# A list that orders the first stage reckons with shorter TensorE turns and scores

## The chip, the cores and the metric

The kernel runs on one core of a Trainium2 chip. The metric is the time of one execution on the device, in microseconds. Three runs of the kernel before took 1630.80, 1632.95 and 1636.01 us; their median is 1632.95.

The engines are named as in the profile: PE is TensorE, which multiplies matrices (PEld its loading of weights), DVE is VectorE, ACT is ScalarE, POOL is GpSimd and SP is SyncE. ACT, POOL and SP also issue transfers between the chip's memory and the on-chip buffers.

## The reference

Attention over keys and values that are means of eight rows, and then two layers:

```python
k_p = k.reshape(B, H, Sp, pool, D).mean(axis=3)      # 576 rows -> 72
v_p = v.reshape(B, H, Sp, pool, D).mean(axis=3)
scores = scale * np.matmul(q, k_p.transpose(0, 1, 3, 2))
attn = np.exp(scores - max) ; attn = attn / (attn.sum() + 1e-09)
x = np.matmul(attn, v_p)                             # 8 batches, 8 heads, 576, 64
x = x.transpose(0, 2, 1, 3).reshape(4608, 512)
h = np.maximum(x @ w_in, 0.0)                        # 512 -> 2048
x = h * h @ w_out                                    # 2048 -> 512
h = x @ w2_in                                        # 512 -> 2048
out = np.maximum(0.01 * h, h) @ w2_out               # 2048 -> 512
```

All data are 32-bit floats; q and k are drawn eight times larger than v.

## The kernel before

A number enters a matrix product as a high and a low part, so that a product is three matmuls: high by high, high by low and low by high. The program has three stages, and the change lies in the first.

**The first stage** (0 to 564 us of the span) computes the attention and the first product of layer 1, block by block: nine blocks of 512 tokens. For a block, q comes in tiles of 128 tokens. TensorE turns a tile of q (L716), multiplies it with the turned, pooled keys (the scores, L764, in two halves), DVE takes the maximum (L774), ACT the exponentials (L786), DVE divides by the sums (L803 to L805) and copies the last keys (L819); TensorE turns the probabilities (L846, the last keys L853), ACT and DVE split these into high and low (L857/L860, L870/L875), and four kinds of value products (L919 to L922) give x, which ACT and DVE split again (L931/L935). The keys of each batch are pooled by DVE, turned by TensorE (L580, the last ones L586) and copied out (L592, L594); the values are pooled (L507), their rest is summed on TensorE (L532), and before they are used DVE puts their three splits into the buffers v_hi, v_lo and v_rem (L650), of which there is one each. Since 576 is no multiple of 512, a block has parts ("pieces") of two batches, and a tile can lie across both.

Then come sixteen **units** for each block: a unit is twelve matmuls of 128x512 (L1064) in four parts of three, into one of four accumulator banks (acc). ACT takes its relu (L1075) and its square (L1078), POOL stores it (L1094), and DVE adds the squares of neighbours (L1101), which POOL stores too (L1104). All other TensorE results pass through four banks named ps.

In the same stage forty **stored** jobs bring the weights of the later products into the form in which they are used: ACT takes an exponent (L242), DVE four bit steps (L246, L249, L260, L263), an addition (L1581) and sums into the single buffer wo3 (L429), which POOL writes out (L431). At its end it loads and splits the eight weight tiles of the next stage (L1767, L1773 on ACT, L1775 on DVE) and prepares three of its groups of tokens (L1736, L1754, L1758).

**What sets the order.** Each engine runs its instructions in the order of its list, and waits where a result or a buffer is not there. The first 16 units and the attention around them are issued by hand. Everything later in the stage, from about 110 us on, is put in order by the planner (`Plan.run`): each step has an engine, an estimated duration in us, a rank, the steps it follows and the buffers it takes. The planner takes, again and again, the step that can start earliest by its own clock (and among those the one of the lowest rank: values and chains of work first, then probabilities, scores, turns, pooling, sums, units, and the stored jobs last), gives it that start, and moves the engine's clock on by its duration. Its clock serves only for the order. The estimates are the second argument of `self.op`.

**The later stages**: the second product of layer 1 (L1800, 564 to about 900 us), in groups of tokens, each prepared by sums (L1736), a cast on ACT (L1754) and low parts on DVE (L1758); and layer 2 (L2021, then L2264), to the end of the span. The change does not touch their order.

Of the kernel before, what the change touches and what calls it, by code (L numbers as in the profile page):

```python
# [45 lines left out]
def attention_relu2_leaky_kernel(  # L46
# [109 lines left out]
    def taken(key):  # L156
        raws.pop(key)
# [1157 lines left out]
    class FirstStage:  # L1315
# [25 lines left out]
        def add_keys(self, b, rank):  # L1341
            rows, tail, kp, km, kl, kt = (
                Buffer(t) for t in ("wo4", "raw", "kp", "gh", "km", "kt")
            )
            load = self.dma(
                lambda: load_to(("k", b, "rows"), k_load_all(b), "wo4", (P, 4, 512)),
                rank, self.ROWS, gets=[rows])
            load_tail = self.dma(
                lambda: load_to(("k", b, "tail"), k_load(b, KEYS // P), "raw"), rank, self.TAIL, gets=[tail])
            steps = []  # L1350
            x = load
            for n, us in enumerate((1.22, 0.69, 0.43)):
                def fn(n=n):
                    if n == 0:
                        steps.extend(k_pool_rows(b))
                    steps[n]()
                after = [x, self.scored.get(b - 2)] if n == 0 else [x]
                x = self.op("DVE", us, fn, rank, after=after, gets=[kp] if n == 0 else (), uses=[rows, kp])
            y = self.op("DVE", 1.03, lambda: k_pool_tail(b), rank, after=[load_tail, x], uses=[tail, kp])
            masks = []  # L1360

            def mask(n):
                if n == 0:
                    masks.extend(k_mask_parts(b))
                masks[n]()

            x = self.op("DVE", 0.68, lambda: mask(0), rank, after=[x, y], gets=[km, kl], uses=[kp])
            y = self.op("DVE", 0.28, lambda: mask(1), rank, after=[x, y], uses=[kp, kl])
            parts = []

            def turn(n):
                if n == 0:
                    parts.extend(k_transpose_parts(b))
                parts[n]()

            p0, p1 = Buffer("ps"), Buffer("ps")
            t0 = self.op("PE", 0.63, lambda: turn(0), rank, after=[x, y], gets=[p0, kt], uses=[km])
            c0 = self.op("DVE", 0.69, lambda: turn(1), self.CHAIN, after=[t0], uses=[p0, kt])
            t1 = self.op("PE", 0.2, lambda: turn(2), rank, after=[y, t0], gets=[p1], uses=[kl])
            c1 = self.op("DVE", 0.22, lambda: turn(3), self.CHAIN, after=[t1, c0], uses=[p1, kt])  # L1380
            self.keys[b] = [c0, c1], kt

# [58 lines left out]
        def add_attention(self, blk):  # L1441
            t0 = blk * T
            self.last = []
            probabilities, pbuf = [], Buffer("pt")
# [5 lines left out]
            before = None  # L1450
            for i in tiles:
                for b, *_ in parts_of(i):
                    if b not in keyed:
                        keyed.add(b)
                        self.add_keys(b, self.POOLING)
                two = len(parts_of(i)) - 1
                raw, qt, ps = Buffer("raw"), Buffer("qt"), Buffer("ps")
                x = self.dma(lambda i=i: load_to(("q", i), q_load(i), "raw"), self.POOLING, self.QUERY,
                             n=1 + two, gets=[raw])
                qp = q_transpose_parts(i)  # L1460

                def copy(i=i, fn=qp[1]):
                    fn()
                    taken(("q", i))

                x = self.op("PE", 0.6, qp[0], 3, after=[x, self.tile.get(i - 2)], gets=[ps, qt], uses=[raw])
                x = self.op("ACT", 0.58, copy, self.CHAIN, after=[x], uses=[ps, qt])
                s, l, m = Buffer("s"), Buffer("l"), Buffer("m")
                after = [x]
                for b, *_ in parts_of(i):  # L1470
                    after += self.keys[b][0] if b in self.keys else []
                kts_ = [self.keys[b][1] for b, *_ in parts_of(i) if b in self.keys]
                exps = []
                for hf in range(2):
                    products, top, ex = score_parts(i, hf)
                    bank_ = Buffer("ps")
                    x = self.op("PE", 0.65 * (1 + two), products, 2, after=after,
                                gets=[bank_] + ([s, l, m] if hf == 0 else []), uses=[qt, *kts_])
                    self.tile[i] = x
                    for b, *_ in parts_of(i):  # L1480
                        self.scored[b] = x
                    after = [x]
                    y = self.op("DVE", 0.46, top, self.CHAIN, after=[x], uses=[bank_, m])
                    exps.append(self.op("ACT", 1.2, ex, self.CHAIN, after=[y], uses=[bank_, s, l, m]))
                whole, last_keys = normalize_parts(i)
                prem = Buffer("prem")
                x = self.op("DVE", 1.15, whole, self.CHAIN, after=exps, uses=[s, l])
                y = self.op("DVE", 0.36, last_keys, self.CHAIN, after=[x], gets=[prem], uses=[s])
                pe, high, low, pe_rem, high_rem, low_rem = p_parts(i, blk)
                b0, b1 = Buffer("ps"), Buffer("ps")  # L1490
                x = self.op("PE", 0.6, pe, 1, after=[x, y, before], gets=[b0] + ([] if before else [pbuf]),
                            uses=[s, pbuf])
                before = x
                h = self.op("ACT", 0.6, high, self.CHAIN, after=[x], uses=[b0, pbuf])
                lo = self.op("DVE", 0.69, low, self.CHAIN, after=[h], uses=[b0, pbuf])
                x = self.op("PE", 0.19, pe_rem, 1, after=[x, y], gets=[b1], uses=[prem])
                hr = self.op("ACT", 0.46, high_rem, self.CHAIN, after=[x], uses=[b1, pbuf])
                lr = self.op("DVE", 0.42, low_rem, self.CHAIN, after=[hr], uses=[b1, pbuf])
                probabilities.append([lo, lr])
            x_buf = self.x_buf[blk] = Buffer(f"x{blk % 2}")  # L1500
            ready = [[] for _ in range(KC)]
            for nb, b in enumerate(batches_of(t0)):
# [4 lines left out]
                for cc in range(KC):  # L1507
                    products, high, low = value_parts(blk, o, e - o, cc)
                    ps = Buffer("ps")
                    share = (e - o) / T  # L1510
                    x = self.op("PE", 4 * (0.0133 + (e - o) / 2400), products, 0,
                                after=[*need, *placed],
                                gets=[ps] + ([x_buf] if nb == cc == 0 else []), uses=[pbuf, vbuf, x_buf])
                    need, placed = [], [x]
                    y = self.op("ACT", 0.17 + 0.42 * share, high, self.VALUES, after=[x], uses=[ps, x_buf])
# [866 lines left out]
```

## Time and profile before

| | us |
|---|---|
| three runs | 1630.80, 1632.95, 1636.01 |
| the profiled execution | 1633.06 |
| its span | 1631.3 |
| TensorE busy | 1614.8 (99%) |
| VectorE busy | 1266.7 (78%) |
| ScalarE busy | 839.2 (51%) |
| GpSimd busy | 189.7 (12%) |
| mean granted clock of TensorE | 0.999 |

Busy times are sums of instructions on one engine; the span runs from the first to the last instruction. A busy share is a mean over stages that have different limits. The table of waits says for whom an engine stood, and with which instruction; the timeline lists instructions in order of their start. The duration of an instruction reaches over the start of the next on the same engine, since they are pipelined; so the distance between two starts is given where instructions follow one another, and the duration where something else waits for the end.

### The profile page before, as it was taken

The numbers are of one execution on the slowest core, as the hardware profiler recorded it, in microseconds if no ns is written. First come the engines' busy times: TensorE is split into PE (matmuls) and PEld (weight loads), VectorE is DVE, ScalarE is ACT, GpSimd is POOL, SyncE is SP. The second block draws the span as 40 slices with busy tenths as digits, with TensorE's granted clock in tenths as the row PEclk, the third lists the DMA queues.
The fourth block names the chain that finished last, engine by engine and source line by source line (L and its number), as shares of the span: only waits on it lengthen the run. The fifth ranks groups of instructions, "written<-read, shape, count | busy, mean of one in ns | idle before, by whom it ended". The sixth has DMA issues, their size and how long they took to land.

```text
span 1631.3 us, 26794 instructions
## 1 busy us (share of the span) xinstructions
PE 1614.8 (99%) x9552; PEld 1463.5 (90%) x9552; DVE 1266.7 (78%) x2244; ACT 839.2 (51%) x1827; POOL 189.7 (12%) x316
## 2 busy tenths in 40 slices
PE   8999999999999999999999999999999999999998
PEld 6788888888888888988888999999999999999998
DVE  6997899987674787887779887887677866666665
ACT  5767776676665653443435543443445533333332
POOL 2112332442334301000000000000000000000000
PEclk9999999999999999999999999999999999999999
DMA  9737777775666994766667757556548744444453
GB/s 247 255 114 227 232 232 224 249 226 199 212 240 213 347 336 158 227 236 220 219 220 250 271 178 247 192 170 230 186 162 285 226 156 156 155 156 156 158 158 104
DMA packets 246581, 343.70 MB, mean 211 GB/s; under 512 B 55344, under 2 KB 173360, under 8 KB 246448
## 3 DMA queue, kind: packets, MB, share of 16 engines
q1 hardware_dynamic: 206016, 249.68, 47.3%
q0 software_dynamic: 21248, 67.65, 11.4%
q10 hardware_dynamic: 19184, 24.66, 5.0%
q8 instruction: 75, 1.23, 0.3%
q14 instruction: 58, 0.48, 0.1%
HBM read 206.66 MB, written 135.27 MB: 210 GB/s over the span
## 4 chain that ended last, share of the span: by engine, by line
PE 88%; DVE 5%; issue 3%; ACT 2%; DMA 1%; POOL 1%; SPq 0%; DVEq 0%; ACTq 0%; POOLq 0%
PE acc L1064 19%; PE ps L2264 11%; PE acc L2264 11%; PE ps L2021 11%; PE acc L2021 11%; PE acc L1800 10%; PE ps L1800 10%; PE ps L764 2%; PE ps L716 1%; PE ps L846 1%; PE ps L922 1%; PE ps L921 1%; PE ps L920 1%; PE ps L919 1%; ACT s L786 0%
## 5 line engine op out<-in xcount | busy, mean ns | idle before, releaser
L1064 PE MATMUL acc<-xh,wi 128*128 128x512 f32 x640 | 220.8, 402 | 0.5 <-ACT st L1075 0.3
L1064 PE MATMUL acc<-wo,wi 128*128 128x512 f32 x704 | 190.5, 399 | 0.0
L1064 PEld LDWEIGHTS acc<-wo,wi 128*128 128x128 f32 x704 | 129.0, 188 | 25.6 <-issue 0.6
L1064 PEld LDWEIGHTS acc<-xh,wi 128*128 128x128 f32 x640 | 120.1, 188 | 26.1 <-ACT st L1075 0.7
L1064 PE MATMUL acc<-xl,wi 128*128 128x512 f32 x320 | 125.0, 391 | 0.0
L2264 PE MATMUL ps<-wi,hh 128*128 128x256 f32 x512 | 93.9, 283 | 0.0
L2264 PE MATMUL acc<-wi,hh 128*128 128x256 f32 x496 | 91.1, 283 | 0.0
L2264 PE MATMUL ps<-wo,hh 128*128 128x256 f32 x496 | 90.9, 283 | 0.0
L2264 PE MATMUL acc<-wo,hh 128*128 128x256 f32 x484 | 88.8, 283 | 0.0
L1754 ACT CAST mh<-ms 128x512 fp32r<-128x512 f32 (+2 forms) x68 | 52.4, 771 | 69.3 <-DVE ms L1736 69.1
L2021 PE MATMUL acc<-fh,wo 128*128 128x384 f32 x384 | 82.6, 337 | 0.0
L2037 ACT ACTIVATE gh<-gh 128x384 f32<-128x384 f32 x48 | 25.3, 527 | 111.1 <-DVE gh L2034 111.1
L2021 PE MATMUL ps<-fh,wi 128*128 128x384 f32 x384 | 82.2, 336 | 0.0
L786 ACT ACTIVATE s<-ps,m 128x72 f32<-128x72 f32 x240 | 74.3, 338 | 14.1 <-DVE m L774 12.0
L2264 PEld LDWEIGHTS ps<-wi,hh 128*128 128x128 f32 x512 | 79.9, 192 | 0.0
L2264 PEld LDWEIGHTS acc<-wi,hh 128*128 128x128 f32 x496 | 77.4, 192 | 0.0
L2264 PEld LDWEIGHTS ps<-wo,hh 128*128 128x128 f32 x496 | 77.4, 192 | 0.0
L1800 PE MATMUL ps<-mh,wi 128*128 128x512 f32 (+1 forms) x256 | 76.3, 363 | 0.1
L1800 PE MATMUL acc<-mh,wi 128*128 128x512 f32 (+1 forms) x256 | 76.0, 362 | 0.0
L2264 PEld LDWEIGHTS acc<-wo,hh 128*128 128x128 f32 x484 | 75.5, 192 | 0.0
L1075 ACT ACTIVATE r<-acc 128x512 f32<-128x512 f32 x88 | 53.3, 607 | 41.4 <-PE acc L1064 40.0
L2264 PE MATMUL ps<-wi,hl 128*128 128x256 f32 x256 | 72.4, 283 | 0.0
(376 smaller groups left out, 4541.3 us busy)
## 6 DMA issues: line engine op xcount, KB each, us to landing
h<-r POOLq DMA_DIRECT2D x88, 256.0 KB, 3.3
hf<-r SPq DMA_DIRECT2D x96, 192.0 KB, 2.7
ml<-h SPq DMA_DIRECT2D x34, 512.0 KB, 3.8
ml<-h SPq DMA_DIRECT2D x59, 256.0 KB, 3.9
hr<-hf SPq DMA_DIRECT2D x23, 640.0 KB, 4.5
xl<-hf SPq DMA_DIRECT2D x23, 640.0 KB, 4.9
xh<-hf SPq DMA_DIRECT2D x23, 640.0 KB, 5.0
h<-st POOLq DMA_DIRECT2D x56, 256.0 KB, 4.2
```

The source lines that it names most:

```text
L716: nc.tensor.transpose(ps[0][:, cc * P : (cc + 1) * P], raw[:, cc * P : (cc + 1) * P], ident)
L764: nc.tensor.matmul(ps[: r0 + n, c2 * PAIR : (c2 + 1) * PAIR], lhsT=qt[:, cc, : r0 + n], rhs=kts[b][:, keys], start=True, stop=True,)
L786: nc.scalar.activation(out=s[:, g, :], in_=at["ps"][:, h * SP : (h + 1) * SP], func=AF.Exp, bias=m[:, g : g + 1], accum_out=l[:, g : g + 1],)
L846: nc.tensor.transpose(ps[:, cc * P : (cc + 1) * P], flat[:, cc * PAIR : cc * PAIR + P], ident)
L919: nc.tensor.matmul(ps, lhsT=v_hi[:, cc, :], rhs=part(ph), start=True, stop=False)
L1064: nc.tensor.matmul(acc_of[blk, c], lhsT=(wih, wil)[w][c][:, kc], rhs=xsplit[blk][x][kc], start=(kc, n) == order[0], stop=(kc, n) == order[-1],
L1075: nc.scalar.activation(out=r, in_=ps, func=AF.Relu)
L1754: nc.scalar.copy(hi[:, at], y)
L1800: nc.tensor.matmul(at[s][:, :n], lhsT=w[:, wx, b, s * P : (s + 1) * P], rhs=x[:, a], start=g % PAIRS == 0 and m == 0, stop=g % PAIRS == PA ...
L2021: nc.tensor.matmul(at, lhsT=w[:, FORMS[j], kc], rhs=x[j][:, kc], start=m == 0 and j not in (4, 6), stop=m == 5, skip_group_check=True,)
L2037: nc.scalar.activation(out=out_, in_=x, func=AF.Lrelu)
L2264: nc.tensor.matmul(at[:, s * TR : (s + 1) * TR], lhsT=x[:, a, s * P : (s + 1) * P], rhs=w[:, b], start=p == 0 and s == 0 and m == 0, stop= ...
```

## The change

Six estimated durations of TensorE steps are made shorter: the turn of the keys from 0.63 to 0.44 us, of the last keys from 0.2 to 0.11, of q from 0.6 to 0.44, the scores from 0.65 to 0.49 (twice that where a tile lies across two batches), the turn of the probabilities from 0.6 to 0.44 and of the last keys in them from 0.19 to 0.11. No instruction is added or taken away. The two lines that weigh most:

```diff
-                x = self.op("PE", 0.6, qp[0], 3, after=[x, self.tile.get(i - 2)], gets=[ps, qt], uses=[raw])
+                x = self.op("PE", 0.44, qp[0], 3, after=[x, self.tile.get(i - 2)], gets=[ps, qt], uses=[raw])
...
-                    x = self.op("PE", 0.65 * (1 + two), products, 2, after=after,
+                    x = self.op("PE", 0.49 * (1 + two), products, 2, after=after,
```

With other durations the planner puts the steps of all engines in another order. Two places show how.

**Place 1, the boundary of the third and the fourth block.** TensorE's list before; acc are units, v_hi, v_lo and v_rem the splits of v, ps a bank, and the number behind a name counts buffers:

```order
L586 MATMUL ps_2871<-cst_78,km_2726 128x64
L1064 MATMUL acc0_2873<-wo6_2188,wi2_580 128x512
L1064 MATMUL acc0_2873<-wo7_2189,wi2_580 128x512
L1064 MATMUL acc0_2873<-wo6_2188,wi2_580 128x512
L1064 MATMUL acc3_2758<-wo6_2188,wi1_483 128x512
L1064 MATMUL acc3_2758<-wo7_2189,wi1_483 128x512
L1064 MATMUL acc3_2758<-wo6_2188,wi1_483 128x512
L919 MATMUL ps_2888<-pth_2472,v_hi_80 128x256
L920 MATMUL ps_2888<-pth_2472,v_lo_81 128x256
L921 MATMUL ps_2888<-ptl_2473,v_hi_80 128x256
L922 MATMUL ps_2888<-ptr_2474,v_rem_82 128x256
L1064 MATMUL acc1_2894<-wo6_2188,wi2_580 128x512
```

TensorE's list now, from the last unit products in front of the values; the next unit product stands 21 rows behind the last row shown:

```order
L1064 MATMUL acc3_2729<-wo6_2147,wi1_483 128x512
L1064 MATMUL acc3_2729<-wo7_2148,wi1_483 128x512
L1064 MATMUL acc3_2729<-wo6_2147,wi1_483 128x512
L919 MATMUL ps_2834<-pth_2518,v_hi_80 128x256
L920 MATMUL ps_2834<-pth_2518,v_lo_81 128x256
L921 MATMUL ps_2834<-ptl_2519,v_hi_80 128x256
L922 MATMUL ps_2834<-ptr_2520,v_rem_82 128x256
L580 MATMUL ps_2840<-cst_78,gh_2603 128x128 x4
L716 MATMUL ps_2849<-cst_78,raw_2529 128x128 x4
L716 MATMUL ps_2854<-cst_78,raw_2686 128x128 x4
L586 MATMUL ps_2874<-cst_78,km_2604 128x64
L919 MATMUL ps_2884<-pth_2518,v_hi_80 128x256
```

Before, units stand on both sides of each group of value products; now value products, turns and scores follow one another with no unit among them.

VectorE's list before, where the splits of v for the next piece are put in place (L650):

```order
L935 TENSOR_TENSOR xl_2712<-ps_2775,xh_2711 128x256
L246 TENSOR_SCALAR gl_2819<-wo1_2096 128x512
L249 SCALAR_TENSOR_TENSOR gl_2819<-wo1_2096,gl_2819 128x512
L650 TENSOR_SCALAR v_hi_80<-vh_2492,cst_78 128x4x64 x2
L935 TENSOR_TENSOR xl_2712<-ps_2814,xh_2711 128x256
L650 TENSOR_SCALAR v_lo_81<-vp_2347,cst_78 128x4x64 x2
L774 TENSOR_REDUCE m_2836<-ps_2837 128x4
L650 TENSOR_SCALAR v_rem_82<-vr_2389,cst_78 96x2x64 x2
L592 COPY kt_2844<-ps_2845 128x512
```

VectorE's list now, at the same splits:

```order
L260 TENSOR_SCALAR wo1_2178<-gl_2751 128x512
L263 SCALAR_TENSOR_TENSOR wo1_2178<-wo1_2178 128x512
L246 TENSOR_SCALAR gl_2831<-wo0_2637 128x512
L249 SCALAR_TENSOR_TENSOR gl_2831<-wo0_2637,gl_2831 128x512
L803 TENSOR_SCALAR l_2756<-l_2756 128x8
L804 RECIPROCAL l_2756<-l_2756 128x8
L805 TENSOR_TENSOR s_2755<-s_2755,l_2756 128x576
L935 TENSOR_TENSOR xl_2704<-ps_2834,xh_2703 128x256
L650 TENSOR_SCALAR v_hi_80<-vh_2508,cst_78 128x4x64 x2
L819 COPY prem0_83<-s_2755 128x64 x2
L650 TENSOR_SCALAR v_lo_81<-vp_2352,cst_78 128x4x64 x2
L592 COPY kt_2839<-ps_2840 128x512
```

The splits stood among two bit steps, two low parts of x (xl) and one maximum; now four bit steps, the normalization of a tile and one low part stand ahead of them, and the copy of the keys (kt) stands among them.

**Place 2, the end of the first stage.** POOL's list before; gl and wo3 are stored forms, r and st squares of units, gh their sums:

```order
L419 DMA w2o_75<-gl_5951 128x128
L420 DMA w2o_75<-gl_5951 128x2x128
L1094 DMA h1_77<-r_5991 128x512
L431 DMA w2o_75<-wo3_6000 128x4x128
L1104 DMA h1_77<-gh_6012 128x512
L1094 DMA h1_77<-st_6029 128x512
L1094 DMA h1_77<-r_6042 128x512
L1104 DMA h1_77<-gh_6058 128x512
L1094 DMA h1_77<-st_6068 128x512
```

POOL's list now, from the same stored form on:

```order
L1094 DMA h1_77<-r_6029 128x512
L419 DMA w2o_75<-gl_6019 128x128
L420 DMA w2o_75<-gl_6019 128x2x128
L1104 DMA h1_77<-gh_6060 128x512
L1094 DMA h1_77<-st_6058 128x512
L431 DMA w2o_75<-wo3_6069 128x4x128
L1094 DMA h1_77<-r_6077 128x512
L1104 DMA h1_77<-gh_6083 128x512
L1094 DMA h1_77<-st_6093 128x512
```

The last output of a stored form, from wo3, stood behind the store of the eleventh of the last block's sixteen units (r_5991) and stands behind that of the fourteenth (st_6058) now.

## Rows read from the trace of the kernel before

**Rows 1.** The page's busy times of the whole span.

```profile
PE 1614.8 (99%) x9552; PEld 1463.5 (90%) x9552; DVE 1266.7 (78%) x2244; ACT 839.2 (51%) x1827; POOL 189.7 (12%) x316
```

**Rows 2.** TensorE's waits, 110 to 564 us: total, times, longest.

```profile
PE ps L853 <- DVE ptr L875: 1.0, 1, 1.0
PE ps L716 <- DVE ptl L860: 0.5, 1, 0.5
...
PE acc L1064 <- ACT st L1075: 0.3, 1, 0.3
```

**Rows 3.** Windows: PE, PEld, DVE, ACT, POOL busy, granted clock, DMA share, GB/s.

```profile
250.00:275.00 25.00, 25.00 (x138) 20.79 (x137) 23.34 (x61) 14.79 (x56) 4.81 (x8) 1.00 0.78 247
```

**Rows 4.** Timeline of TensorE around 250 us: start, duration, engine, line, operation.

```profile
246.54 1.04 PE L716 MATMUL ps<-cst,raw 128*128 128x128 f32 x8
247.34 0.95 PE L1064 MATMUL acc<-wo,wi 128*128 128x512 f32 x3
248.12 0.28 PE L919 MATMUL ps<-pth,v_hi 128*128 128x256 f32 x1
...
248.59 1.55 PE L1064 MATMUL acc<-wo,wi 128*128 128x512 f32 x6
...
256.44 1.29 PE L764 MATMUL ps<-kt,qt 128*128 128x144 f32 x8
```

**Rows 5.** Timeline of VectorE in the same stretch.

```profile
248.93 0.42 DVE L246 TENSOR_SCALAR gl<-wo 128x512 uint32<-128x512 uint32 x1
...
249.99 0.61 DVE L650 TENSOR_SCALAR v_hi<-vh,cst 128x256 fp32r<-128x256 f32 x2
...
252.73 1.21 DVE L507 TENSOR_TENSOR wo<-wo 128x1024 f32<-128x1024 f32 x1
253.86 0.45 DVE L774 TENSOR_REDUCE m<-ps 128x4 f32<-128x288 f32 x1
254.23 0.21 DVE L594 COPY kt<-ps 128x64 f32<-128x64 f32 x1
...
256.99 0.42 DVE L935 TENSOR_TENSOR xl<-ps,xh 128x256 fp32r<-128x256 f32 x1
257.33 0.29 DVE L819 COPY prem<-s 128x64 f32<-128x64 f32 x2
```

**Rows 6.** The page's group of the exponentials: busy, mean ns of one.

```profile
L786 ACT ACTIVATE s<-ps,m 128x72 f32<-128x72 f32 x240 | 74.3, 338 | 14.1 <-DVE m L774 12.0
```

**Rows 7.** Timelines around the stage's end, and the issues of wo from 525 us.

```profile
556.88 0.77 POOL L431 DMA_DIRECT2D w2o<-wo  x1 [0.32 <-DVE ml L1758]
562.41 0.54 POOL L1094 DMA_DIRECT2D h<-st  x1 [1.47 <-ACT st L1078]
561.47 2.05 ACTq L1767 DMA_DIRECT2D wo<-w1o  x2
567.26 2.29 ACT L1773 CAST wo<-wo 128x768 fp32r<-128x768 f32 x3
571.29 0.69 DVE L1736 TENSOR_TENSOR ms<-xl 128x512 f32<-128x512 f32 x1
573.82 1.23 DVE L1758 TENSOR_TENSOR xl<-ms,mh 128x1024 fp32r<-128x1024 f32 x1 [0.51 <-ACT mh L1754]
576.50 0.39 PE L1800 MATMUL ps<-xl,wo 128*128 128x512 f32 x1
wo<-w1o ACTq DMA_DIRECT2D x6, 384.0 KB, 5.0
```

**Rows 8.** Timelines: the longest waits of ScalarE near 537, of VectorE near 340.

```profile
536.61 1.05 ACT L1773 CAST wi<-wi 128x1024 fp32r<-128x1024 f32 x1 [5.37 <-DMA wi<-w1o]
339.59 0.42 DVE L429 TENSOR_TENSOR wo<-gl 128x256 f32<-128x256 f32 x1 [2.46 <-DMA w1o<-wo]
```

**Rows 9.** Windows of the first 34 us.

```profile
5.00:20.00 15.00, 11.86 (x57) 7.32 (x56) 9.80 (x15) 8.23 (x38) 2.99 (x3) 1.00 1.11 294
30.00:34.00 4.00, 3.79 (x20) 3.83 (x21) 3.36 (x11) 2.01 (x4) 1.43 (x3) 0.57 0.62 158
```

More of the change, by code (lines that the diff above doesn't have):

```diff
@@ L1376, in add_keys @@
             p0, p1 = Buffer("ps"), Buffer("ps")
-            t0 = self.op("PE", 0.63, lambda: turn(0), rank, after=[x, y], gets=[p0, kt], uses=[km])
+            t0 = self.op("PE", 0.44, lambda: turn(0), rank, after=[x, y], gets=[p0, kt], uses=[km])
             c0 = self.op("DVE", 0.69, lambda: turn(1), self.CHAIN, after=[t0], uses=[p0, kt])
-            t1 = self.op("PE", 0.2, lambda: turn(2), rank, after=[y, t0], gets=[p1], uses=[kl])
+            t1 = self.op("PE", 0.11, lambda: turn(2), rank, after=[y, t0], gets=[p1], uses=[kl])
             c1 = self.op("DVE", 0.22, lambda: turn(3), self.CHAIN, after=[t1, c0], uses=[p1, kt])
@@ L1490, in add_attention @@
                 b0, b1 = Buffer("ps"), Buffer("ps")
-                x = self.op("PE", 0.6, pe, 1, after=[x, y, before], gets=[b0] + ([] if before else [pbuf]),
+                x = self.op("PE", 0.44, pe, 1, after=[x, y, before], gets=[b0] + ([] if before else [pbuf]),
                             uses=[s, pbuf])
@@ L1495, in add_attention @@
                 lo = self.op("DVE", 0.69, low, self.CHAIN, after=[h], uses=[b0, pbuf])
-                x = self.op("PE", 0.19, pe_rem, 1, after=[x, y], gets=[b1], uses=[prem])
+                x = self.op("PE", 0.11, pe_rem, 1, after=[x, y], gets=[b1], uses=[prem])
                 hr = self.op("ACT", 0.46, high_rem, self.CHAIN, after=[x], uses=[b1, pbuf])
```

## The prediction

> **What bounds the kernel now.** I read the busy times first: TensorE works 1614.8 us of the span [rows 1], so the kernel ends when TensorE's list ends, and what another order can do is only to add or take away time in which TensorE stands. The table of TensorE's waits comes next, over the stretch that the changed list orders (110 to 564 us). It is short: 1.0 us at a turn of the last keys and 0.5 at a turn of q right behind it, both for VectorE, twice 0.3 at a unit's first product for ScalarE [rows 2], and one of 0.3 more. All of it is under 2.5 us, 0.15% of the time. The matmuls are the same before and after in number and kind; so a gain of more than those 2.5 us has no place to come from, and the question is which new waits the new list makes. Last I read VectorE in the stretch where the fourth block follows the third: of 25 us it works 23.34 while TensorE works all 25 [rows 3]. Wherever TensorE would wait for a chain of VectorE steps there, nothing is in reserve.
>
> **What the change does to the orders.** Six estimates of TensorE steps become shorter by a quarter to a half. They remove and add no instruction. In the list's own clock the turns and scores pass sooner, so the list believes that TensorE has more time for units before VectorE's next result; it issues the units of a block earlier, and at two places it has none left.
>
> Place 1 is the boundary of the third and fourth block. Before, units stand between all parts of the attention: the last values of one piece of the block and the first of the next have eighteen unit products between them. In the new order five groups of value products, twelve square turns and a small one, two scores of eight records each and the sum of the rest follow one another, and no unit product stands among them. TensorE's work in them, by the starts of like rows: five value groups of 0.47 (248.12 to 248.59), 13 turns of 0.10 (eight from 246.54 to 247.34), two scores of 1.29, and the rest taken as one more 0.47, together 2.35 + 1.30 + 2.58 + 0.47 = 6.7 us [rows 4]. These steps pass through four accumulator banks that VectorE and ScalarE must empty, and the values of the next piece need the three splits of its v, which may only be written when the last value product of the piece before has been read. So VectorE's own list sets the end: it must go through, in its order, a maximum (0.37, 253.86 to 254.23), two pairs of bit steps for the stored weights (1.06 each, 248.93 to 249.99), the normalization with the pooling of its shape (254.23 to 256.99, 2.76, of which some 0.3 is a last pooling step that stands later in the new list), two lows of x (0.34 each, 256.99 to 257.33), the copy of the last keys (0.29), the three splits with the keys' copy (249.99 to 252.73, 2.74, less a low and a maximum that lie in it, 2.03), the pooling of 1024 columns (1.13, 252.73 to 253.86), one more pooling step on 32 partitions (0.3 by its width) and the second maximum (0.37) [rows 5]. That is 0.37 + 2.12 + 2.46 + 0.68 + 0.29 + 2.03 + 1.13 + 0.3 + 0.37 = 9.75 us. The first maximum can begin nine unit products before the stretch, 9 x 0.26 = 2.3 us (three from 247.34 to 248.12). So the second maximum is done 7.4 us into the stretch; four exponentials of 338 ns follow on ScalarE [rows 6], 8.8 us, then the rest and the last values on TensorE, 0.94: the stretch ends at 9.7 us and holds 6.7 us of work. The wait is 3.0 us by starts. By full durations (a row of VectorE is some 0.08 longer than the distance to the next start, 0.42 against 0.34 at 256.99; 25 instructions lie on the path) it is 2.0 more, 5.0. Back to back the starts count, behind each wait for another engine the whole duration does; I take the middle, **4.0**. The lower end is 1: the two pairs of bit steps (2.1) wait for no TensorE step of this stretch, and a VectorE that is ahead of the list does them before. The upper end is 7: VectorE has 1.7 us to spare in 25 [rows 3], and if it comes some 2 us late to the stretch, all of that is added to the 5.0.
>
> Place 2 is the end of the first stage. The first layer's second product works through groups of tokens. Three groups are prepared inside the list; ScalarE and VectorE prepare the fourth (tile xl) only when they have split the last three of the eight weight tiles, wo0, wo1 and wo3. The load of wo3 waits until the last stored form has been read out of the single buffer of that name (L431). In the new order the last sums and this output stand behind the 14th unit's store on POOL's queue. Before, the output started at 556.88 and ScalarE's queue let the load go at 561.47 + 2.05 = 563.5, which is 6.6 us later. The 14th unit's store of before started at 562.41 and took 0.54; an output behind it starts at 563.0, the load goes at 569.6, and lands by the median of 5.0 at 574.6. Then follow one cast (2.29 / 3 = 0.76), one low part (three fill the time from the first cast's end to 571.29, (571.29 - 567.26 - 0.76) / 3 = 1.1) and the preparation of the fourth group, which in this trace took from 571.29 to 573.82 + 1.23 = 575.05, 3.76 us: 574.6 + 5.6 = 580.2. TensorE took the first product with that group's low part at 576.50 [rows 7]. So TensorE would wait 3.7 us. If the output lands a microsecond sooner, as the POOL queue carries less by then, it is 2.7. I take **2.9**, with ends of 0 (ScalarE's queue issues the load before, the store of the 14th unit is earlier) and 4. The later groups are prepared ahead of TensorE again, so this is paid once.
>
> What goes. ScalarE's wait of 5.37 us for the weight wi at 536.61 held two relus, and through them TensorE twice [rows 2, 8]; in the new list the casts of wi stand behind five casts of wo and three more relus, so that the load has landed: -0.55 (0.29 and 0.26 unrounded). The 1.0 and 0.5 stem from VectorE standing 2.46 us at 339.59 for a store out of the same single buffer [rows 2, 8]. The new list moves the sums of this kind everywhere, but the buffer stays single: I take half of 1.5, **-0.75**, between 0 and -1.5. The 0.3 stays.
>
> The profiled execution took 1633.06 us, beside the median of 1632.95; the sum goes from the former: 1633.06 + 4.0 + 2.9 - 0.55 - 0.75 = 1638.66, say **1638.7**.
>
> At place 1 something speaks for more. Early in the first stage TensorE stood three times within four microseconds for results of the same kind, and from 30 to 34 us its granted clock was 0.57 of 2.4 GHz, that is mostly at the lower level of 1.2; (1 - 0.57) x 4 = 1.7 us were lost [rows 9]. From 5 to 20 us TensorE stood more, with 11.86 of 15 us busy, and the clock stayed whole [rows 9]. The Trainium skill, page "TensorE: Matmul & The Clock Gate", section "A second HAM failure mode: psum-queue depth-cycling", says that a TensorE which idles briefly and often between groups of matmuls while it goes round its accumulator banks has its clock swing between half and full. Place 1 would be such a stretch, and by that rule the sum is 1640.4; this trace shows the fall once and other stretches without it, so the rule is a rival below and not in the sum.
>
> **The rivals.** The clock falls at place 1: three to five waits on banks within ten microseconds, as at 30 us. For it speaks the fall in the trace, against it the stretches without one, and that TensorE comes from a long time of full work. Price +1.7: 1640.4.
>
> VectorE comes late to place 1, as it is 93% busy there: 7 instead of 4.0, and the stage end at 3.7: 1633.06 + 7 + 3.7 - 0.55 = 1643.2.
>
> Not slower: the list's gaps are in the list's clock, not the chip's. VectorE has done its bit steps before the stretch (from 2.1 us ahead on it decides), and the wait is 1; the last output is earlier by as much as the units are earlier, so the load of wo3 is in time and the stage end costs 0 to 1; the removed waits give back 0.55 to 1.3. 1633.06 + 1 + 0.5 - 1.2 = 1633.4. For it speaks that TensorE's waits in this stretch are so few that VectorE must have run ahead most of the time; against it the 93%.
>
> Only what goes: neither place waits, and all 2.05 us go: 1631.0. For it speaks only that scores and turns really are as short as the new numbers say, so that the list is nearer to the chip; against it that the list that ran with the long numbers left next to nothing to gain.
>
> **How the numbers follow.** The kernel's runs differ by about 0.3% (4.9 us), which I take for the least that can be told from no change: faster is under 1628.05, slower over 1637.85. The forecast has 0.48; its own range, with 2 to 5.5 at place 1 and 1.5 to 3.5 at place 2, is 1635.5 to 1641, of which two thirds lie above the bound: slower 0.33, same 0.15. Clock 0.12, all slower. VectorE late 0.10, all slower. Not slower 0.24, all same. Only what goes 0.06, of which 0.03 is set apart as faster for what no row shows. Together slower 0.55, same 0.42, faster 0.03. The range of 8 in 10 leaves out half of the last two rivals at each end: 1632.5 to 1643.
>
> **What would show it.** Place 1: a wait table of TensorE from 250 to 275 us with value products, scores or the rest behind VectorE, 3 to 5 us together, and a stretch of about ten without a unit; wrong if they stay under 1.5. Place 2: TensorE waits once, near 580, at L1800 for the low part xl of the fourth group, and the last output on POOL starts behind the 14th unit's store; wrong if the first product with that low part starts within 0.5 us of its predecessor. The clock: a window of four microseconds under 0.9 behind place 1. What goes: no wait at L1064 for ScalarE near 538; the 1.5 near 341 halved or moved. The whole is wrong if TensorE's waits from 110 to 600 us sum to less than they did before, or if the time changes while these waits do not.

## The result and the profile after

Six runs of the changed kernel have a median of 1644.07 us (1641.82 to 1646.48), beside 1633.2 of the kernel before in six; the ratio is 1.0066 with an interval of 1.0053 to 1.0079. It is slower by some 11 us. The prediction, 1638.7 with a range to 1643, had the side right and the size wrong.

The page of the changed kernel, its busy times (as [rows 1]):

```profile
span 1643.3 us, 26795 instructions
PE 1618.8 (99%) x9552; PEld 1467.0 (89%) x9552; DVE 1266.7 (77%) x2244; ACT 841.9 (51%) x1827; POOL 189.0 (11%) x316
```

TensorE's matmuls are the same; it is busy 4 us longer, having run some of them at the lower clock (windows below). Its waits from 110 to 620 us (total, times, longest), which answer to [rows 2]:

```profile
PE ps L1800 <- ACT mh L1754: 8.1, 1, 8.1
PE ps L919 <- DVE v_hi L650: 0.7, 1, 0.7
PE ps L1800 <- DVE xl L1758: 0.5, 1, 0.5
PE ps L920 <- DVE v_lo L650: 0.3, 1, 0.3
PE ps L922 <- DVE v_rem L650: 0.3, 1, 0.3
PE ps L586 <- ACT qt L725: 0.2, 1, 0.2
```

All waits of before are gone, and two places stand in their stead: one wait of 8.1 us at L1800, the end of the first stage, with 0.5 behind it, and 1.5 us in small waits at place 1, of which 1.3 are for v's splits (v_hi, v_lo, v_rem). The windows of the two places (core's time, then busy time of PE, PEld, DVE, ACT and POOL, the granted clock, DMA share, GB/s), as [rows 3]:

```profile
254.00:256.00 2.00, 1.30 (x11) 0.93 (x9) 1.93 (x8) 1.20 (x3) 0.00 (x0) 1.00 0.10 24
256.00:258.00 2.00, 1.24 (x6) 0.86 (x7) 2.00 (x10) 0.00 (x0) 0.00 (x0) 1.00 1.14 244
258.00:260.00 2.00, 2.00 (x12) 1.51 (x11) 2.00 (x3) 0.37 (x1) 0.00 (x0) 0.71 0.02 3
260.00:262.00 2.00, 2.00 (x10) 1.71 (x9) 2.00 (x7) 1.09 (x6) 0.00 (x0) 0.50 0.00 0
...
580.00:584.00 4.00, 0.00 (x0) 0.00 (x0) 1.56 (x2) 1.35 (x2) 0.00 (x0) 0.50 1.06 398
584.00:588.00 4.00, 1.70 (x3) 1.10 (x4) 3.42 (x5) 1.57 (x2) 0.00 (x0) 0.50 0.31 121
588.00:592.00 4.00, 4.00 (x15) 3.14 (x15) 3.41 (x5) 1.57 (x2) 0.00 (x0) 0.76 0.00 0
```

At place 1 VectorE is busy throughout, and TensorE falls to the lower clock (0.50) from about 258.8 us on; at the stage's end the DMA engines are full (share 1.06) while TensorE stands, and it starts again at the lower clock.

To see what each place costs in the whole, I add up TensorE's work in each trace, every instruction at the median time from start to start of its kind in the trace of before, and compare the times at which equal amounts are done. So much later than before is TensorE (us; positions by the work done, which lies near the time in the trace of before):

| kernel | at 220 | from 220 to 300 (place 1) | 300 to 500 | 500 to 540 | 540 to 580 (stage's end) |
|---|---|---|---|---|---|
| changed | +1.0 | +3.3 | -1.9 | -1.1 | +10.7 |
| early_stored | -0.7 | +3.3 | -2.0 | -1.1 | +0.1 |
| late_stored | -0.7 | +1.0 | -1.9 | 0.0 | +11.7 |
| own_buffer | -0.3 | +3.1 | -1.9 | -1.1 | +9.1 |
| own_buffer_prefetch | -0.5 | +3.4 | -2.0 | -1.1 | +12.4 |
| fed | +1.2 | +3.1 | -2.0 | -1.1 | +9.3 |
| loads_free | +1.0 | +3.4 | -2.0 | -1.1 | 0.0 |
| loads_on_sp | +0.5 | +3.3 | -1.9 | -1.1 | 0.0 |
| short_bits | +1.2 | +2.4 | -1.9 | -1.1 | +1.2 |
| no_small_turns | -1.3 | +2.4 | -1.7 | -0.5 | +17.1 |
| keys_only | +0.8 | 0.0 | -1.9 | -1.1 | 0.0 |
| both_mended | -1.1 | +0.1 | -1.8 | -1.1 | +5.7 |
| clean | +0.1 | -0.2 | -1.7 | -1.1 | +7.0 |
| clean_26 | 0.0 | -0.3 | -1.5 | -1.1 | +11.9 |

The column at 220 is the scatter of single executions: it lies between -1.3 and +1.2 with no pattern; late_stored, whose order at place 1 is that of before, has +1.0 there, so an entry is good to about 1 us. At the end it is good to some 3 us only: own_buffer and own_buffer_prefetch ask for the three loads from the same place, and have +9.1 and +12.4. The column from 300 to 500 is -1.5 to -2.0 everywhere, in late_stored too, whose order there is that of before: the wait of 1.5 us near 341 [rows 2, 8] was a matter of that one execution, and no gain of the change. The changed kernel's own costs are 3.3 at place 1 and 10.7 at the end, and 1.1 near 538 comes back (its profiled execution, 1645.07 us, is 1.0 above its median).

The end in the changed kernel, from ScalarE's, POOL's, VectorE's and TensorE's timelines, as [rows 7]:

```profile
566.72 0.76 POOL L431 DMA_DIRECT2D w2o<-wo  x1 [1.92 <-DVE ms L1736]
567.39 7.28 ACTq L1767 DMA_DIRECT2D wo<-w1o  x3
575.33 0.84 ACT L1773 CAST wo<-wo 128x768 fp32r<-128x768 f32 x1 [6.89 <-DMA wo<-w1o]
578.09 0.83 ACT L1773 CAST wo<-wo 128x768 fp32r<-128x768 f32 x1 [1.93 <-DMA wo<-w1o]
581.55 0.83 ACT L1773 CAST wo<-wo 128x768 fp32r<-128x768 f32 x1 [2.63 <-DMA wo<-w1o]
585.83 0.79 PE L1800 MATMUL ps<-mh,wo 128*128 128x512 f32 x1 [8.12 <-ACT mh L1754]
```

All three loads are asked for at 567.4 or later, 6.5 us after the first of them before (560.84). The first lands at 575.3, so wo0 alone took 8 us, the other two come 2.8 and 3.5 later. From the last cast to TensorE's first product of the fourth group pass 4.28 us; they are 4.28 in late_stored too (578.41 to 582.69) and 4.29 in own_buffer (578.28 to 582.57), so the wait is set by when wo3 lands.

### The profile page after: what moved, and what is told of

It reads as the page before. It is cut to its first block, busy times and chain, and to the rows that moved or that the text cites. A ratio compares the mean times of both kernels' runs of the same rounds, so it can differ in the third digit from the quotient of the medians.

```text
span 1643.3 us, 26795 instructions
## 1 busy us (share of the span) xinstructions
PE 1618.8 (99%) x9552; PEld 1467.0 (89%) x9552; DVE 1266.7 (77%) x2244; ACT 841.9 (51%) x1827; POOL 189.0 (11%) x316
## 4 chain that ended last, share of the span: by engine, by line
PE 90%; DVE 5%; DMA 2%; issue 1%; ACT 1%; SPq 0%; DVEq 0%; ACTq 0%
PE acc L1064 23%; PE ps L2264 11%; PE acc L2264 11%; PE acc L2021 10%; PE ps L2021 10%; PE ps L1800 9%; PE acc L1800 9%; PE ps L764 2%; PE ps L846 1%; PE ps L716 1%; DMA xh<-h 1%; PE ps L919 1%; PE ps L922 1%; PE ps L921 1%; PE ps L920 1%
## 5 line engine op out<-in xcount | busy, mean ns | idle before, releaser
L1064 PE MATMUL acc<-xh,wi 128*128 128x512 f32 x640 | 220.1, 402 | 0.0
L1064 PE MATMUL acc<-wo,wi 128*128 128x512 f32 x704 | 190.1, 398 | 0.0
L1064 PEld LDWEIGHTS acc<-wo,wi 128*128 128x128 f32 x704 | 129.3, 188 | 25.4 <-issue 0.4
L1064 PEld LDWEIGHTS acc<-xh,wi 128*128 128x128 f32 x640 | 120.8, 189 | 24.8 <-DVE wi L306 0.2
L1064 PE MATMUL acc<-xl,wi 128*128 128x512 f32 x320 | 125.6, 393 | 0.0
L786 ACT ACTIVATE s<-ps,m 128x72 f32<-128x72 f32 x240 | 74.2, 336 | 11.3 <-DVE m L774 10.1
L1800 PE MATMUL ps<-mh,wi 128*128 128x512 f32 (+1 forms) x256 | 76.2, 363 | 0.1
L1800 PE MATMUL acc<-mh,wi 128*128 128x512 f32 (+1 forms) x256 | 76.0, 362 | 0.0
L1800 PE MATMUL ps<-mh,wo 128*128 128x512 f32 (+1 forms) x224 | 67.9, 365 | 8.1 <-ACT mh L1754 8.1
```

What stands on the lines that cost most here:

```text
L786: nc.scalar.activation(out=s[:, g, :], in_=at["ps"][:, h * SP : (h + 1) * SP], func=AF.Exp, bias=m[:, g : g + 1], accum_out=l[:, g : g + 1],)
L1064: nc.tensor.matmul(acc_of[blk, c], lhsT=(wih, wil)[w][c][:, kc], rhs=xsplit[blk][x][kc], start=(kc, n) == order[0], stop=(kc, n) == order[-1],
L1800: nc.tensor.matmul(at[s][:, :n], lhsT=w[:, wx, b, s * P : (s + 1) * P], rhs=x[:, a], start=g % PAIRS == 0 and m == 0, stop=g % PAIRS == PA ...
```

## The experiments

Each is timed against the kernel before on the same chip, and its ratio is to that. late_stored changes the kernel before, no_small_turns and keys_only hold only a part of the six durations, the others start from the changed kernel.

**early_stored** and **late_stored** move only the last stored jobs, in the list's own terms.

```diff
-                x.ready = self.STORED_AT + h * self.STORED_EVERY
+                x.ready = self.STORED_AT + h * self.STORED_EVERY - (8.0 if h > 35 else 0.0)
```

and in late_stored

```diff
+                x.ready = self.STORED_AT + h * self.STORED_EVERY + (12 if h == STORED_EARLY - 1 else 0.0)
```

> The changed kernel with the last four stored jobs let into the list 8 us earlier; place 1 stands as in the changed kernel, and at the stage's end the last output of a stored form stands seven unit stores from the end (two in the changed kernel, five before). Theory: the stage's end alone makes 10.8 of the changed kernel's loss, so it goes to 1633.5 us (1632 to 1636), no wait over 1 us at L1800, and a TensorE that is 3 to 4 us later behind place 1 as in the changed kernel. Rival: place 1 and what it pushes back carry the loss; then 1638 or more is left.

> The kernel before, its last stored job alone let into the list 12 us later; the order up to the last block is that of before, and the stage's end is that of the changed kernel (two unit stores behind the last output, the three loads of wo behind all units). Theory: the stage's end costs by itself what it costs in the changed kernel, 10.8 us: 1644 (1642 to 1646), one wait of about 8 us at L1800 near 577 and a granted clock at the lower level behind it. Rival: the wait is so long only because TensorE, having come through the stage with fewer waits, outran the rest; then 1636 to 1639.

early_stored: 1634.87 us, 1.0013 (1.0004 to 1.0021). late_stored: 1642.31, 1.0056 (1.0043 to 1.0070), with TensorE's waits from 110 to 620 us led by the same one:

```profile
PE ps L1800 <- ACT mh L1754: 7.9, 1, 7.9
```

So the stage's end alone makes the kernel before about as slow as the changed one, and taking it away leaves the changed kernel 2 us over before. The rivals of both are out.

**own_buffer** takes away the wait of wo3's load for the last output, the mechanism of the prediction.

```diff
-                sums, steps = Buffer("wo3"), []
+                own = "raw" if h == STORED_EARLY - 1 else "wo3"; sums, steps = Buffer(own), []
```

(and `own` in place of "wo3" where the sums are made)

> The changed kernel, its order untouched, but the last stored sums lie in a buffer of q (raw) instead of wo3, so that the load of wo3 need not wait for their output. Theory: that wait is the cause; wo3 is asked for near 568 behind wo0 and wo1 and lands near 575 instead of 581.5; TensorE waits 2 to 3 us, the clock stays; 1636.5 (1634.5 to 1638.5). Rival: the late place of all three loads, behind the last casts and in front of the next groups' loads on full DMA engines, is enough: wo3 lands near 579.5, the wait is 6 us and the clock falls; 1641 to 1642.5.

1644.25, 1.0068 (1.0056 to 1.0080): nothing gained against the changed kernel's 1.0066, and above the range of the rival too. The trace shows why:

```profile
564.38 0.76 POOL L431 DMA_DIRECT2D w2o<-raw  x1 [1.47 <-DVE gh L1101]
565.50 0.34 ACTq L1767 DMA_DIRECT2D wo<-w1o  x1
565.88 2.53 ACTq L1767 DMA_DIRECT2D wo<-w1o  x2
573.72 0.83 ACT L1773 CAST wo<-wo 128x768 fp32r<-128x768 f32 x1 [7.00 <-DMA h<-gh]
576.48 0.83 ACT L1773 CAST wo<-wo 128x768 fp32r<-128x768 f32 x1 [1.93 <-DMA wo<-w1o]
578.28 0.83 ACT L1773 CAST wo<-wo 128x768 fp32r<-128x768 f32 x1 [0.97 <-DMA wo<-w1o]
```

wo3 is asked for at 568.4 (565.88 + 2.53), 6.3 us sooner than in the changed kernel (567.39 + 7.28), and still lands only 3.3 sooner, about 10 us after the request; TensorE's wait is 6.4 us in this execution, the fastest of its five (1641.76). The theory fell: the rival, that the late place of all three loads is enough, holds for the mechanism.

**fed** asks what the lower clock behind the wait costs.

```diff
+                for _ in range(32 if g == 3 and j == 0 else 0):
+                    nc.tensor.matmul(self.banks[6], lhsT=w[:, 0, a, :P], rhs=self.old, start=True, stop=True)
+                self.old = hi[:, 0]
```

> The changed kernel with 32 needless matmuls of 128x512 (into a bank that is free then) between the third and the fourth group, 7.3 us of work inside the wait of 8.1. Theory: the clock stays at its upper level, and the 2.0 us that TensorE lost at the lower one behind the wait come back: 1642.0 (1641 to 1643). Rival: the lower clock costs nothing there, since VectorE's low parts set the pace: no change, 1644. If the wait were shorter than the trace shows, the kernel would be slower.

1642.94, 1.0064 (1.0052 to 1.0076), beside the changed kernel's 1.0066 (1.0053 to 1.0079): the intervals overlap, so the time does not settle it. The window behind the wait does for the clock:

```profile
584.00:588.00 4.00, 2.51 (x11) 1.52 (x10) 3.42 (x5) 1.57 (x2) 0.00 (x0) 1.00 0.28 111
```

The clock stayed whole, and from the first product of the fourth group to the next group passed 5.25 us (585.64 to 590.89) instead of 6.57 (585.83 to 592.40). The clock costs 1.3 us there; VectorE's low parts took back the rest (0.8 of wait).

**loads_free** leaves the stored form late and moves the loads.

```diff
-                        after = both if p in (0, 1, 3) else attention
+                        after = attention + (self.stored_adds[{3: "wo3"}.get(p, p)] if p in (0, 1, 3) else [])
```

(stored_adds holds the last users of the buffers wo0, wo1 and wo3; the last two sums lie in raw)

> The changed kernel with the loads of wo0, wo1 and wo3 tied in the list each to the last user of its own buffer instead of to the whole set of stored jobs (the last two stored sums lie in a buffer of q). Ten units and more stand behind the loads of wo0 and wo1, one behind that of wo3; in the changed kernel none. Place 1 and the steps up to the last block stand as in the changed kernel; the last stored form is written one unit store later than there. Theory now: what costs at the stage's end is that all three loads are asked for behind the last cast, when the next groups' loads fill the DMA engines; then no wait over 1.5 us at L1800 and 1635 us (1633.5 to 1637), as with the stored jobs let in earlier. Rival: the late stored form itself holds the end up (its output, and its bit steps on VectorE and ScalarE); then a wait of 4 us or more, 1640 or more.

1634.54, 1.0010 (1.0001 to 1.0019), no wait at L1800 up to 620 us, and place 1 as in the changed kernel: the theory's number. wo0 and wo1 were there long before, and wo3, asked for alone at 565.68, landed by 571.8, 6 us instead of 10.

**loads_on_sp** is the sharper form. It starts from own_buffer: the list, ScalarE's order and the late stored form stay, only the queue that asks is another.

```diff
-            queue = nc.sync if four else nc.scalar
+            queue = nc.sync if four or p in (0, 1, 3) else nc.scalar
```

> The kernel own_buffer (order of the changed kernel, last stored sums in a buffer of q), with the three loads of wo0, wo1 and wo3 issued by SyncE instead of ScalarE. There they stand ahead of the loads of the fourth and fifth group (563.8 us in own_buffer) and wait only for their buffers, not behind ScalarE's last units and casts. Theory: the place on ScalarE's list is what costs; the loads are asked for near 563 and land near 570 instead of 573.7 to 578.3, ScalarE casts them by 572, TensorE waits under 2 us at L1800 and the clock stays: 1636 us (1634.5 to 1638). Rival: the amount that is moved then is what costs, whoever asks first; the groups' loads come as much later, the wait stays over 4: 1640 or more.

1634.46, 1.0016 (1.0007 to 1.0025). SyncE had asked for the loads by 563.0 (562.02 + 0.94), ahead of the groups' loads, and ScalarE cast all three in one go:

```profile
562.02 0.94 SPq L1767 DMA_DIRECT2D wo<-w1o  x2
564.75 0.37 SPq L1721 DMA_DIRECT2D xl<-h  x1
568.24 2.30 ACT L1773 CAST wo<-wo 128x768 fp32r<-128x768 f32 x3
```

The wait is gone by moving three requests to another queue; own_buffer, in an earlier session, took 9.8 us more. With own_buffer's own edit, this is the shortest mend of the changed kernel.

**own_buffer_prefetch** starts from own_buffer too, and was to show that the loads are slow because they share full DMA engines with the next groups' loads.

```diff
-            return (4, 2) if n < 0 else (2, 1)
+            return ((3, 2) if 5 <= g <= 7 else (4, 2)) if n < 0 else (2, 1)
```

> The kernel own_buffer, with the loads of the sixth to eighth group asked for one group later (4.1 us), so that 0.77 MB less stands beside the loads of wo. Theory: those share full DMA engines (about 0.4 MB a us); wo3 lands 1.5 to 2 us sooner than there (578.3), TensorE's wait falls from 6.4 to about 4.5; 1642 us (1641 to 1643). Rival: the loads of wo take their 8 us by their own queue, whatever the other queue moves: the wait stays and 1644.

1644.1, 1.0066 (1.0052 to 1.0079), no change; but the edit did not do what it says. The loads of ml (the sixth group and on) were asked for at 567.88 and 571.96, in own_buffer at 567.84 and 571.92: they wait for their buffer, which the first groups free at the same time, and not for their place in the list. Only the eighth group's load went later (578.80 for 576.00), and a load of wi went in its stead (574.01 for 578.89). So it tells nothing of sharing.

**no_small_turns** leaves the two shortest durations (0.2 and 0.19) as they were.

> Four of the six durations changed; the two of the last keys' turns (0.2 and 0.19) stay as before. In this order place 1 is gone (no stretch without a unit is longer than before), and the stage's end is as late as in the changed kernel (all three loads of wo behind the last unit, the last stored form behind all unit stores). Theory: place 1's 3.4 us go, the stage's end stays at 10 to 12, the removed waits give back 2 to 3: 1641.5 us (1639.5 to 1643.5), no waits at L919 for VectorE near 256. Rival: the two places are one thing (who is late at place 1 is late at the end); then the end is shorter and 1637 or less.

1650.21, 1.0109 (1.0096 to 1.0123). TensorE's waits for v's splits are gone as expected, but not the delay: it waits 1.2 us at L1064 near 236 and 0.6 at L919 near 243, both for ScalarE, and place 1's column has 2.4. And the end costs 17.1 instead of 10 to 12: the last loads are asked for at 569.7 and later, wo3 is cast at 585.66, and TensorE waits 13.3 us at L1800. The same loads are late, and the size follows from the order. Two durations, each changed by less than 0.1 us, decide which waits arise; the effect of all six is nothing that one could scale.

**short_bits** tries place 1 by taking work from VectorE.

```diff
+                    first_bits(st["val"], st["top"], h != 8)
...
+                x = self.op("DVE", 1.12, run(lambda st, h=h: h == 7 or low_term(st["val"], st["top"], st["low"])), R,
```

(job 8 without L249, job 7 without L260, L263 and its addition L1581, so that their stored forms are not computed; elsewhere as early_stored)

> The kernel early_stored, with three of the four bit steps that stand at place 1 on VectorE left out (1.66 us; the stored forms of two jobs are not computed rightly). Nothing else of the order moves. Theory: VectorE's list sets the length of place 1, so TensorE's delay there (3.4 us in the traces of the changed kernel and of early_stored) falls to about 1.8, and the time by as much, 1633.2. Rival: TensorE at the lower clock sets the length, or the waits on banks; then the delay stays at 3 or more and the time at 1634.9.

1634.1, 1.0007 (0.9998 to 1.0016), beside early_stored's 1634.87 in another session: not told apart. The traces tell more: from the first of the five value groups to the next unit product pass 9.9 us (253.26 to 263.1) instead of 10.9, the delay falls from 3.3 to 2.4. But the clock stayed whole in this execution and fell in early_stored's; beside own_buffer and fed, where it stayed too and the same stretch takes 10.5, 0.7 of the 1.66 us taken from VectorE arrive. The rest goes to waits for the exponentials: VectorE itself stands 1.05 us at L803, and TensorE 0.97 at L532, the last step of the prediction's chain. VectorE's list does set the end of place 1, but not by itself.

**keys_only, clean, clean_26 and both_mended** look for a better kernel and for a third cause. keys_only changes the first line of the diff alone, with the loads as in loads_free. The other three have all six durations, with the loads as in loads_free (clean, clean_26) or loads_on_sp (both_mended), and stored jobs at other times, by which place 1 does not arise.

```diff
-        STORED_AT, STORED_EVERY = 25.0, 10.3
+        STORED_AT, STORED_EVERY = 25.0, 10.2
```

(clean; in clean_26 26.0 and 10.3 with 0.6 * max(0, h - 25) off for job h, in both_mended 25.0 and 10.1)

> All six new durations, the loads of wo tied as in loads_free, and the stored jobs let in every 10.2 instead of 10.3 us, with which place 1 does not arise. Theory: with both places gone only the removed waits are left of the change, 2 to 3 us: 1630.5 (1629 to 1632.5). Rival: the new order has further small costs that the two places cover; then 1634 or more.

> All six new durations, the loads of wo tied as in loads_free, the stored jobs let in from 26 instead of 25 us on and the last fourteen a little sooner each. In this order place 1 does not arise, ten, three and two units stand behind the loads of wo, and two unit stores behind the last stored form (none in the kernel clean). Theory: only the removed waits are left, about 3 us: 1630.2 (1629 to 1632). Rival: as in the kernel clean, the late last stored job holds up the preparation of the third group on VectorE, 4 us or more at L1800: 1635.

> Of the six durations only that of the keys' turn (0.63 to 0.44), the loads of wo tied as in loads_free. No stretch without a unit is longer than in the kernel before, four unit stores stand behind the last stored form. Theory: neither place arises, so the time is that of the kernel before within 2 us: 1632 (1630.5 to 1634). Rival: shorter durations cost by themselves, through VectorE running later against TensorE; then 1635 or more.

> All six new durations; the last stored sums in a buffer of q and the three loads of wo issued by SyncE, as in loads_on_sp; the stored jobs let in every 10.1 us, with which place 1 does not arise (no stretch without a unit is longer than before) and the last stored form stands as late as in the changed kernel. Theory: the change consists of place 1 (3.4 us), the place of the loads (9 to 11 us) and removed waits (2 to 3 us given back); with the first two gone 1630 us (1629 to 1632). Rival: a late stored job costs by itself (as in the kernels clean and clean_26, by the third group's preparation on VectorE); then 1634 or more, with a wait for ml or mh at L1800.

clean: 1636.99, 1.0026 (1.0015 to 1.0037). clean_26: 1639.95, 1.0047 (1.0033 to 1.0060). both_mended: 1635.99, 1.0021 (1.0012 to 1.0030). keys_only: 1631.51, 0.9994 (0.9986 to 1.0003), not told apart from before, as its theory said. In clean and both_mended the rivals were right; in clean_26 only their time was: TensorE's waits there are others (2.2 us at L1064 for ScalarE, 2.6 at L1800), and their cause is open. both_mended shows the third cause best. TensorE was 3.9 us ahead of before at 540 (1.8 of them the wait near 341), and then (POOL's, VectorE's and TensorE's timelines):

```profile
569.19 0.76 POOL L431 DMA_DIRECT2D w2o<-raw  x1 [5.27 <-issue]
569.97 0.69 DVE L1101 TENSOR_TENSOR gh<-r,st 128x512 f32<-128x512 f32 x1 [3.16 <-DMA h<-gh]
570.58 1.22 DVE L1758 TENSOR_TENSOR ml<-ms,mh 128x1024 fp32r<-128x1024 f32 x1
571.85 0.50 PE L1800 MATMUL ps<-ml,wo 128*128 128x512 f32 x1 [2.74 <-DVE ml L1758]
```

A sum of squares waits for the store out of the buffer gh, and the third group's low parts wait behind that sum on VectorE. In clean the same two waits are 4.75 us on VectorE and 5.23 on TensorE. That it is the late stored job that costs in this third way, through POOL's stores, is argued and not shown: in loads_on_sp the last stored form stands as late, VectorE waits 0.89 us for the same store, and TensorE, 4.7 us further back at 540, waits for nothing; an early TensorE may only meet what is not ready yet. Of the 2.2 us by which keys_only leads in its trace, 1.8 are the wait near 341; a kernel clearly faster than the one before was not found.

## Why the prediction was wrong

- **What bounds the kernel** held: TensorE's work is the same, and the loss is new waits. That no more than 2.5 us could be gained held in all kernels.
- **Place 1** held: forecast 4.0, measured 3.3, at the place named, with VectorE busy throughout from 256 to 262. That it is so near is partly luck, as 4.0 was the middle of two readings (3.0 and 5.0), and the sign set for it was a poor one: TensorE's waits behind VectorE there sum to 1.3 us, under the 1.5 that was to prove it wrong. The delay is seen in the stretch: from the first of the five value groups to the next unit product 10.96 us pass (253.08 to 264.04), with some 6.4 us of work in them. The clock, a rival at +1.7, fell as it said, and cost 0.4: with the same order it fell to 0.50 in the changed kernel, early_stored, loads_free, loads_on_sp and own_buffer_prefetch, and the stretch takes 10.9 to 11.0 us; it stayed at 1.00 in own_buffer and fed, and the stretch takes 10.5. There TensorE waits 1.0 us at L532 for the exponentials, in the other five not at all: where VectorE sets the pace, a slower TensorE mostly fills its waits. The Trainium skill ("TensorE: Matmul & The Clock Gate", "A second HAM failure mode: psum-queue depth-cycling") says that a TensorE which idles often between groups of matmuls while it goes round its banks has its clock swing, and that throughput suffers by it. The clock fell in five of these seven executions, and the throughput suffered by 0.4 us in 11.
- **What goes** was half right. The waits near 538 went (1.1 with what hung on them, forecast 0.55). The 1.5 near 341, half of which was counted, was no property of the order: late_stored, with the old order, does not have it.
- **Place 2** is the step that failed: forecast 2.9 with an upper end of 4, measured 10.7 (9 to 12 in the kernels with the same end). The step had only wo3 late, behind L431, and took the loads' median landing of 5.0 us from a stretch in which they had been asked for one after another, before the groups' loads. In the trace L431 came 3.7 us later than reckoned (566.7 against 563.0: the 14th unit's store 1.9 later, then 1.9 in which POOL waited for VectorE), its landing took 1.3 more, wo3's landing 1.9 more (6.9). With these sizes the step's own chain gives 580.2 + 6.9 = 587.1 for the first product with the fourth group's low part, and the trace has it at 587.09: the chain was there, with three of its terms too small. But the cost does not hang on it, since own_buffer, without any wait for L431, is no faster (1.0068 beside 1.0066). In the new order all three loads stand on ScalarE's list behind the last unit's square and the third group's casts. They are asked for after the loads of the fourth and fifth group, and from 572 to 584 us the DMA engines move 398 to 411 GB/s with a share of 1.03 to 1.06. early_stored, loads_free and loads_on_sp show that asking earlier takes the whole cost away, and late_stored that asking later brings it.
- **The clock behind the wait** had no place in the prediction: after eight us of standing TensorE starts at 1.2 GHz, and 1.3 us are lost to that (fed).

Why the loads are slow was not settled by an experiment: the one that was to hold the groups' loads back hardly moved them. The landings speak for the traffic: the issue table's median for wo<-w1o was 7.2 us in the changed kernel and 10.2 in own_buffer (560 to 582 us), 4.9 in loads_on_sp, where they were asked for first:

```profile
wo<-w1o ACTq DMA_DIRECT2D x3, 384.0 KB, 10.2
...
wo<-w1o SPq DMA_DIRECT2D x2, 384.0 KB, 4.9
```

So do the packets of the queues. ScalarE's queue is q10 and carries only these loads (1.18 MB from 560 to 582 us), POOL's is q0 and SyncE's q1. Packets, MB and share of the engines before from 563 to 567 us, then in own_buffer from 566 to 570 and from 570 to 577:

```profile
q10 hardware_dynamic: 374, 1.03, 72.9%
q0 software_dynamic: 123, 0.38, 23.6%
q1 hardware_dynamic: 16, 0.03, 5.4%
...
q1 hardware_dynamic: 573, 1.09, 82.0%
q0 software_dynamic: 85, 0.28, 17.4%
q10 hardware_dynamic: 3, 0.01, 0.9%
...
q10 hardware_dynamic: 372, 1.04, 37.8%
q0 software_dynamic: 315, 1.03, 36.2%
q1 hardware_dynamic: 388, 0.74, 28.2%
```

Before, the loads had most of the engines and moved 1.03 MB in 4 us. In own_buffer, asked for from 565.5 on, they moved next to nothing up to 570, while SyncE's queue, with the groups' loads, moved 1.09 MB; then they took 7 us for 1.04 MB, beside as much of POOL's stores and 0.74 MB of the groups' loads. So the traffic that they share with is POOL's as well as the groups'; why none of them moved before 570 is not shown. The Trainium skill ("Trainium Kernel Development and Optimization", "Key Constraints") says that transfers from SyncE's, ScalarE's and GpSimd's queues run on the same 16 engines and interleave. The last three rows agree with it.

## What to carry to other kernels

A list that is ordered by estimated durations is not made better by truer estimates of a part (five of the six new numbers are nearer to the trace of before, where a turn of q takes 0.35 us and a tile's scores 0.40 by starts; the last keys' turn takes its old 0.20): small numbers move work in steps, and a place where the new order fits badly can cost more than all that the old estimates did. When such an order moves, look first at the requests for transfers, with the queue on which each stands and what is ahead of it there: a load put behind the last computation of its queue comes late twice, by its place and by the traffic that it meets. A price for a transfer is to be taken from a stretch with the same traffic.

## What was not expected of the hardware

- The same loads of 384 KB took 5 us from the request to the landing, or 7 to 12 where they were asked for 3 to 7 us later (medians: 6.8 in late_stored, 11.6 in own_buffer_prefetch).
- A fall of the clock to half speed for 3.4 us lengthened a stretch in which VectorE was busy nearly throughout by only 0.4 us (10.5 without the fall, 10.9 to 11.0 with it).
- With the same order, TensorE's clock fell at place 1 in five of the seven kernels named above, and stayed in two.
